# Retention and two MLPs on one core: tiles of their own for one half-depth product, GpSimd's sums in another order

## The chip, the core and the metric

The kernel runs on one core of a Trainium2 chip. Its engines work side by side, each through its own queue in order: TensorE (PE in the profile) multiplies, VectorE (DVE), ScalarE (ACT) and GpSimd (POOL) do the elementwise work, SyncE (SP) issues the transfers. Semaphores order work between engines. The metric is the device time of one execution in microseconds; lower is better.

## The reference

Per head a state decays and takes in one token; the result, of 1536 tokens by 512, goes through two MLPs with a hidden width of 2048. All is float32.

```
state = gamma * state + k_t v_t^T ;  y_t = q_t state / sqrt(64)     # 2 x 8 heads, 768 tokens, 64 wide
h = x @ w_in ;  g = max(h, 0) + log1p(exp(-|h|)) ;  x = g @ w_out    # layer 0 (softplus)
h = x @ w_in2 ; g = s * max(h, 0)^2 + b ;           y = g @ w_out2   # layer 1
```

## The kernel before

**Products in three parts.** TensorE multiplies a short format, so every operand is split in a high part (ScalarE copies it, rounding) and a low part (GpSimd or VectorE subtracts the high part): wh and wl of the weights, gh and gl of the hidden values, xh and xl of the inputs. A product is high x high, high x low and low x high. Tokens lie in three tiles of 512 (j = 0, 1, 2); the hidden width in 16 blocks of 128. The first product of a block (12 matmuls of 128x512) makes h; the curve makes g; the second product (`acc_mm`, `acc_2`, 12 matmuls into four accumulator banks) adds to the output, and VectorE reads the banks out into xa (`take_2`, L591). The first group's readout is ScalarE's (`take_out`, L412).

**The weights.** `split_w` makes one half of a block's weights from raw words: four VectorE operations in two pairs (L287 and L291, then L296 and L302), a square on ScalarE (L294), and at the next slot wh on ScalarE and wl on GpSimd (L112, L115). An ordered list (`halves`, made by `pair`) says which half comes next; each slot of the program (`part`) takes one from it, up to a limit, and `go(work, 2)` issues it in two pieces.

**Layer 0** runs in this order: twelve steps (blocks 0 to 3 for each j; the last four, 8 to 11, after retention is over), a plain part (`plain`, blocks 4 and 5, six slots k = 0 to 5), three pairs of blocks by `second` (pairs 3, 4, 5), and twelve steps more (36 to 47). Layer 1 is a plain part and seven pairs.

**A pair** (`second`) saves products: with j = 0 and 1 and the two halves of depth it needs seven half-depth products (`six`, 6 matmuls) instead of eight. For these it needs sums of x (x1 to x4, made once by `sum_x0`, split by `parts_x`) and four sums of weights (`sums_w`, ws, on GpSimd; `split_sums` makes sh and sl). Its six slots are, with TensorE's work: (2) two products for c11, second product; (3) two products with sums of weights, second product; (4) two products for c12 and c22, second product; (5) one for c21, second product; (6) 12 matmuls for ha (j = 2), second product; (7) 12 for hb, second product. The second products in (2) to (5) belong to the pair before.

**The curve** of layer 0 in a pair: r = max(h, 0) on ScalarE (`begin`, L534); u = h - 2r = -|h| on VectorE (`middle`, L546); softplus of u on ScalarE (L547); c = r + u on GpSimd (`finish`, L555). The split into gh and gl is issued a slot later (`end_part`). In the plain part and the steps the curve is three operations: VectorE, ScalarE, VectorE (L536, L539, L559 and L360, L366, L370). c and u come from a ring of four tiles (`next_t`: t1 and t2, two each).

Of the kernel before, what the change touches and what calls it, by code (L numbers as in the profile page):

```python
# [7 lines left out]
F32 = mybir.dt.float32  # L8
# [40 lines left out]
def tile_retention_mlps(ctx: ExitStack, tc: tile.TileContext, qk, kv, w1, w2, sb, consts, out):  # L49
# [401 lines left out]
    def sum_x0(k):  # L451

        def of(j, half):
            return [t[j][:, 2 * half : 2 * half + 2].bitcast(F32) for t in (xh, xl)]

        def put(op, to, x, y):
            nc.vector.tensor_tensor(out=to, in0=x, in1=y, op=op)

        add, less = ALU.add, ALU.subtract
        (h11, l11), (h12, l12), (h21, l21), (h22, l22) = of(0, 0), of(1, 0), of(0, 1), of(1, 1)  # L460
        if k > 2:
            h, l = (h22, l22) if k == 3 else (h21, l21)
            for c, tag in enumerate(("p5", "u2")):
                t = x3[c] = late.tile([P, TT], F32, tag=tag, name=tag)
                put(less, t, h[:, c], (h12 if k == 3 else x_t[2])[:, c])
            yield
            for c in range(2):
                put(add, x3[c], x3[c], l[:, c])
                if k == 3:
                    put(less, x3[c], x3[c], l12[:, c])  # L470
            yield
            return
        t = x_t[k] = xa[2][:, 2 * k - 2 : 2 * k]
        put(less, t, h12 if k == 1 else h22, h11 if k == 1 else x_t[1])
        yield
        put(add, t, t, l12 if k == 1 else l22)
        yield
        if k == 1:
            put(less, t, t, l11)
            yield  # L480

    def parts_x(k, la=1):
# [40 lines left out]
        nc.vector.tensor_tensor(out=c, in0=ps, in1=t, op=ALU.add)  # L523
        return c

    def begin(la, src, own=False, by_pool=True):

        if la:
            c = src if own else next_t()
            nc.scalar.activation(c, src, AF.Relu)  # L530
            return src, c, None
        r = next_t()
        if by_pool:
            nc.scalar.activation(r, src, AF.Relu)  # L534
            return src, r, src if own else next_t()
# [76 lines left out]
    def pair(la, p):  # L612
        w = la * NF + 2 * p
        at[la, p] = len(halves)
        if p != (0 if la else P0):
            return [(w, 0), (w + 1, 0), (w, 2), (w, 1), (w, 3), (w + 1, 1)]
        return [(w, 0), (w + 1, 0), (w, 1), (w + 1, 1)]

    for p in range(P0, P1):
# [12 lines left out]
    def load_next():  # L632
        x = next(loads, None)
        if x:
            load_w(*x)

    def split_next(to):
# [5 lines left out]
        if x[1] == 2:  # L643
            return sums_w(x[0])
        if x[1] == 3:
            return split_sums(x[0])
# [62 lines left out]
    with tc.manual_schedule():  # L709
# [146 lines left out]
        def plain(la, p, left, sums, parts):  # L856

            w = la * NF + 2 * p
            base = at[la, p + 1]
            accs = left + [lambda: whole(*of_pair(la, p, 0, 0)), lambda: whole(*of_pair(la, p, 0, 1)), lambda: None]  # L860
            banks = [(ps_h, "h"), (ps_y, "y"), None, (ps_h, "h"), None, (ps_y, "y")]
            for k, (j, half) in enumerate((j, half) for j in range(NTILE) for half in range(2)):
                part(base + k + 2)
                to = bank(*banks[k]) if banks[k] else bank_2[1]
                all_of(to, w_t[w + half, 0], j)
                if la and k == 2:
                    end_part()
                    accs[k]()
                of = begin(la, to, by_pool=False)
                if not la:  # L870
                    end_part()
                    go(work, 2)
                finish(la, p, half, j, of)
                if la:
                    end_part()
                if not la or k != 2:
                    accs[k]()
                go(work, 4 if la else 2)
                for x in sums[k]:
                    next(x, None)  # L880
                for x in parts[k]:
                    parts_x(x, la)

        def second(la, p):
# [16 lines left out]
            six(third, a12, b21, True)  # L901
            c11 = begin(la, joined(third, p1), own=True)
            end_part()
            go(work, 2)
            middle(c11)
            whole(*of_pair(la, p - 1, 1, 0))
            finish(la, p, 0, 0, c11)
            go(work, 2)

            part(base + 3)  # L910
            six(other, s1, t1, True)
# [1 line left out]
            six(one, s2, t2, False)  # L913
            u2 = kept(one, "u2")
            end_part()
            go(work, 2)
            whole(*of_pair(la, p - 1, 1, 1))
            go(work, 2)

            part(base + 4)  # L920
            six(other, s4, b22, False)
# [4 lines left out]
            go(work, 2)  # L926
# [32 lines left out]
            go(work, 2)  # L959
# [17 lines left out]
        sums_0 = all_x0()  # L977
        for s in range(SB, GS):
            accs = [of_step(s - LAG)]
            step(s, accs, at[0, P0 + 1] * (s < SB + 2), [sums_0] * max(1, s - SB), nc.gpsimd)  # L980
        s = GS - 1
        act_3(s)
        act_hi(s)
        act_lo(s, nc.gpsimd)
        parts_x(1, 0)
        left = [lambda s=s: whole(*of_step(s)) for s in range(GS - LAG, GS)]
        plain(0, P0, left, [[], [], [sums_0], [sums_0], [], []], [(2,), (4,), (), (), (3,), ()])
        for p in range(P0 + 1, P1):
            second(0, p)
        end_part()  # L990
# [103 lines left out]
```

## Time and profile before

| | |
|---|---|
| median of 3 runs | 594.05 us (591.74 to 594.84) |
| the profiled execution | 594.36 us, its span 592.3 us |
| TensorE, VectorE, ScalarE, GpSimd busy | 570.2, 418.7, 337.1, 329.4 us |
| TensorE's granted clock, mean | 0.986 of full speed |

TensorE is the engine that sets the time. A timeline row gives the start, how long the instruction (or a run of like ones, with its count) took, and in brackets the idle time before it with the instruction that ended it. Matmul records overlap: each shows 0.39 us and starts 0.23 after the one before it.

### The profile page before, as it was taken

The page shows a single profiled execution, that of the slowest core. Times are in us where ns is not written, and L with a number is a line of the kernel's source. Part 1 is how long each engine was busy: PE and PEld are TensorE (multiplying, and loading weights), DVE is VectorE, ACT ScalarE, POOL GpSimd, SP SyncE. Part 2 cuts the span into 40 slices and gives each one's busy share as a digit, 9 for nine tenths or more (in the row PEclk, how much of TensorE's full clock was granted, in tenths as well). Part 3 has the DMA queues.
Part 4 walks back from the last instruction along what each step waited for, and adds up shares of the span by engine and source line. Part 5 has one row for each costly group of instructions (what it writes and reads, how often), then busy time and mean ns, then how long its engine had stood idle before and what let it go on. Part 6 is the DMA issues. An engine that isn't in the chain of part 4 may idle for free.

```text
span 592.3 us, 8095 instructions
## 1 busy us (share of the span) xinstructions
PE 570.2 (96%) x2968; PEld 466.6 (79%) x2968; DVE 418.7 (71%) x628; ACT 337.1 (57%) x606; POOL 329.4 (56%) x266
## 2 busy tenths in 40 slices
PE   8889999999969979899999999999999999999997
PEld 7767878877858858688888887888888888888886
DVE  4898768889956749988786778657667575765324
ACT  4655563454544454643253788777666666767470
POOL 3447632767875686761043759846465555647130
PEclk9999999998989989899999999999999999999999
DMA  8986122121212212232121213131212212100005
GB/s 335 413 308 197 48 72 71 37 71 37 71 36 71 71 37 71 82 101 68 35 72 35 72 35 107 36 108 35 89 53 72 72 58 85 37 0 1 0 1 213
DMA packets 14870, 50.58 MB, mean 85 GB/s; under 512 B 1776, under 2 KB 1776, under 8 KB 14832
## 3 DMA queue, kind: packets, MB, share of 16 engines
q1 hardware_dynamic: 14832, 50.08, 24.6%
q8 instruction: 23, 0.38, 0.3%
q14 instruction: 15, 0.12, 0.1%
HBM read 46.93 MB, written 3.15 MB: 85 GB/s over the span
## 4 chain that ended last, share of the span: by engine, by line
PE 56%; POOL 4%; ACT 2%; DVE 2%; issue 1%; DVEq 0%; POOLq 0%; ACTq 0%
PE acc L581 25%; PE h L498 6%; PE acc L404 5%; PE y L506 5%; PE third L506 4%; PE y L498 3%; PE h L353 3%; PE y L353 3%; PE third L498 2%; POOL gl L115 1%; DVE xa L591 1%; POOL c L555 1%; POOL wl L115 1%; PE h L506 0%; ACT c L553 0%
## 5 line engine op out<-in xcount | busy, mean ns | idle before, releaser
L115 POOL TENSOR_TENSOR wl<-wm,wh 128x512 fp32r<-128x512 f32 x64 | 86.4, 1350 | 119.9 <-ACT wh L112 119.9
L115 POOL TENSOR_TENSOR gl<-c,gh 128x512 fp32r<-128x512 f32 x72 | 94.4, 1314 | 101.2 <-ACT gh L112 87.5
L591 DVE TENSOR_TENSOR xa<-acc,xa 128x512 f32<-128x512 f32 x132 | 82.4, 684 | 84.0 <-PE acc L581 83.9
L581 PE MATMUL acc<-wh,gh 128*128 128x512 f32 x192 | 74.9, 390 | 0.0
L581 PE MATMUL acc<-wh,gl 128*128 128x512 f32 x192 | 74.7, 389 | 0.0
L112 ACT ACTIVATE gh<-c 128x512 fp32r<-128x512 f32 x72 | 45.5, 632 | 12.7 <-POOL c L555 8.6
L581 PE MATMUL acc<-wl,gh 128*128 128x512 f32 x192 | 52.5, 389 | 0.0
L581 PE MATMUL acc<-gh,wh 128*128 128x512 f32 x96 | 39.9, 416 | 12.0 <-DVE xa L591 10.2
L112 ACT ACTIVATE wh<-wm 128x512 fp32r<-128x512 f32 x64 | 39.8, 622 | 18.0 <-DVE wm L302 18.0
L294 ACT ACTIVATE wm<-raw 128x512 f32<-128x512 f32 x64 | 42.1, 658 | 2.6 <-POOL ws L321 1.7
L581 PEld LDWEIGHTS acc<-wh,gh 128*128 128x128 f32 x192 | 36.0, 188 | 8.2 <-DVE xa L591 0.4
L302 DVE SCALAR_TENSOR_TENSOR wm<-wm,word 128x512 f32<-128x512 f32 x54 | 37.2, 688 | 7.3 <-ACT wm L294 1.5
L291 DVE SCALAR_TENSOR_TENSOR word<-raw,cu,word 128x512 uint32<-128x512 uint32 x54 | 40.8, 756 | 1.9
L581 PEld LDWEIGHTS acc<-wl,gh 128*128 128x128 f32 x192 | 36.1, 188 | 7.5
L581 PEld LDWEIGHTS acc<-wh,gl 128*128 128x128 f32 x192 | 36.0, 188 | 7.4
L296 DVE SCALAR_TENSOR_TENSOR word<-raw,cu,word 128x512 uint32<-128x512 uint32 x54 | 40.5, 751 | 0.8
L553 ACT ACTIVATE c<-c,sbt 128x512 f32<-128x512 f32 x48 | 39.2, 818 | 1.6
L581 PE MATMUL acc<-gl,wh 128*128 128x512 f32 x96 | 39.9, 416 | 0.0
L404 PE MATMUL acc<-gh,wh 128*128 128x512 f32 x96 | 38.3, 399 | 0.0
L404 PE MATMUL acc<-gl,wh 128*128 128x512 f32 x96 | 37.5, 390 | 0.0
L287 DVE TENSOR_SCALAR word<-raw 128x512 uint32<-128x512 uint32 x54 | 37.1, 687 | 0.4
L530 ACT ACTIVATE c<-c 128x512 f32<-128x512 f32 x21 | 13.3, 633 | 42.0 <-DVE c L523 41.4
(213 smaller groups left out, 1405.0 us busy)
## 6 DMA issues: line engine op xcount, KB each, us to landing
raw<-w SPq DMA_DIRECT2D x64, 512.0 KB, 3.7
qk<-qk SPq DMA_DIRECT2D x12, 512.0 KB, 7.8
kv<-kv SPq DMA_DIRECT2D x12, 512.0 KB, 7.9
out<-xa SPq DMA_DIRECT2D x12, 256.0 KB, 2.1
cst<-consts SPq DMA_DIRECT2D x1, 518.0 KB, 4.2
cst<-consts SPq DMA_DIRECT2D x1, 256.0 KB, 5.4
sbt<-sb SPq DMA_DIRECT2D x1, 1.0 KB, 10.6
```

Source lines behind the costliest of these rows:

```text
L112: nc.scalar.activation(hi, src, AF.Copy)
L115: lo_eng.tensor_tensor(out=lo, in0=src, in1=hi.bitcast(F32), op=ALU.subtract)
L291: nc.vector.scalar_tensor_tensor(out=x, in0=hw, scalar=cu[:, 0:1], in1=x, op0=ALU.bitwise_and, op1=ALU.bitwise_or)
L294: nc.scalar.activation(m, hw.bitcast(F32), AF.Square)
L296: nc.vector.scalar_tensor_tensor(out=x, in0=lw, scalar=cu[:, 1:2], in1=x, op0=ALU.logical_shift_right, op1=ALU.bitwise_or)
L302: nc.vector.scalar_tensor_tensor(out=m, in0=m, scalar=TINY_SQ, in1=x.bitcast(F32), op0=ALU.is_ge, op1=ALU.mult)
L404: nc.tensor.matmul(acc_t[la, g, j][cc], *ops[i], start=f4 == 0 and i == 0, stop=ends(s) and i == 2)
L498: nc.tensor.matmul(ps, w[a][:, k * P : (k + 1) * P], x[b][:, k], start=start and i == 0, stop=i == len(ops) - 1, skip_group_check=True,)
L506: nc.tensor.matmul(ps, w[a][:, k * P : (k + 1) * P], (xh, xl)[b][j][:, k], start=i == 0, stop=i == len(ops) - 1)
L553: nc.scalar.activation(c, c, AF.Identity, scale=sbt[:, 0:1], bias=sbt[:, 1:2])
L581: nc.tensor.matmul(acc_t[la, p, "pair", j][cc], *ops[i], start=half == 0 and i == 0, stop=half == 1 and i == 2)
L591: nc.vector.tensor_tensor(out=dst, in0=ps, in1=dst, op=ALU.add)
```

## The change

c21's two curve tiles no longer come from the ring of four: they lie in the places of u2 and p1, two tiles of the pair that hold copied-out products. GpSimd's sums of weights (`sums_w`, `split_sums`) are issued at the end of a slot, behind the curve's sums, and in layer 0's list the second sum step stands ahead of the second half of a block's weights. The plain part's blocks 0 and 1 take no weights, so all later halves of layer 0 come two slots later; steps 36 to 39 take one in every slot. x's first sum goes from VectorE (three operations of 128x1024) to GpSimd (six of 128x512); x3 is made from x2; x4 and x3 are summed behind blocks 0 and 1. The gl of steps 36 to 39 goes to GpSimd.

```diff
         if k > 2:
-            h, l = (h22, l22) if k == 3 else (h21, l21)
...
+            t, t2 = x3, x_t[2]
+            todo = ((t2, h11, less), (None, l11, less)) if k == 3 else ((h21, t2, less), (None, l21, add))
+            for x, y, op in todo:
+                for c in range(2):
+                    nc.vector.tensor_tensor(out=t[c], in0=t[c] if x is None else x[:, c], in1=y[:, c], op=op)
             return
         t = x_t[k] = xa[2][:, 2 * k - 2 : 2 * k]
         if k == 1:
-            put(less, t, t, l11)
+            for x, y, op in ((h12, h11, less), (t, l12, add), (t, l11, less)):
+                for c in range(2):
+                    nc.gpsimd.tensor_tensor(out=t[:, c], in0=x[:, c], in1=y[:, c], op=op)
+                yield
...
-    def begin(la, src, own=False, by_pool=True):
+    def begin(la, src, own=False, by_pool=True, tags=None):
...
+        if tags:
+            r, u = (late.tile([P, TT], F32, tag=tag, name=tag) for tag in tags)
...
-            return [(w, 0), (w + 1, 0), (w, 2), (w, 1), (w, 3), (w + 1, 1)]
+            return [(w, 0), (w + 1, 0), (w, 2)] + [(w, 1), (w, 3)][:: 1 if la else -1] + [(w + 1, 1)]
...
+        def go_first():
+            if work not in sums_of_w:
+                go(work, 2)
+
+        def go_last():
+            go(work, 4 if work in sums_of_w else 2)
...
-                part(base + k + 2)
+                part(base + k + 2 if la or k > 1 else 0)
...
-            c21 = begin(la, one)
+            c21 = begin(la, one, tags=("u2", "p1"))
             end_part()
-            go(work, 2)
+            go_first()
...
-            step(s, accs, at[0, P0 + 1] * (s < SB + 2), [sums_0] * max(1, s - SB), nc.gpsimd)
+            step(s, accs, at[0, P0 + 1] * (s < SB + 2), [sums_0], nc.gpsimd)
...
-        plain(0, P0, left, [[], [], [sums_0], [sums_0], [], []], [(2,), (4,), (), (), (3,), ()])
+        plain(0, P0, left, [[sums_0], [sums_0], [], [], [], []], [(4,), (2,), (), (3,), (), ()])
...
-            step(s, accs, 0 if k < 4 and k % 2 or k > 4 and ends(s - LAG) else lim)
+            step(s, accs, 0 if k > 4 and ends(s - LAG) else lim, lo=nc.gpsimd if k < 5 else None)
```

Three places show the order of the instructions. ScalarE in pair 4, slots 4 and 5 before (c_2026 and c_2036 are the curves of c12 and c22, c_2074 is c21's tile, h_1918 its product, gh_2077 c12's high part; the brackets name the engines it waits for):

```order
L112 ACTIVATE wh0_1994<-wm_1996 128x512
L547 ACTIVATE c_2026<-c_2026 128x512 [waits DVE_49]
L547 ACTIVATE c_2036<-c_2036 128x512 [waits DVE_49]
L534 ACTIVATE c_2074<-h_1918 128x512 [waits PE_49,Pool_49]
L112 ACTIVATE gh_2077<-c_2028 128x512
```

and now (u2_2056 is c21's tile, h_1897 its product):

```order
L294 ACTIVATE wm_2021<-raw_1759 128x512 [waits DMAHW7_49,Pool_49]
L546 ACTIVATE c_2003<-c_2003 128x512 [waits DVE_49]
L546 ACTIVATE c_2013<-c_2013 128x512 [waits DVE_49]
L533 ACTIVATE u2_2056<-h_1897 128x512 [waits PE_49]
L112 ACTIVATE gh_2059<-c_2005 128x512 [waits Pool_49]
```

c21's first curve instruction no longer waits for GpSimd; c12's high part, behind it, now does.

GpSimd in pair 4 before, from slot 3's weights to the sums' low part (c x2 are c12 and c22, the next c is c21):

```order
L115 TENSOR_TENSOR wl_1945<-wm,wh_1944 128x512
L115 TENSOR_TENSOR wl_1995<-wm,wh_1994 128x512
L321 TENSOR_TENSOR ws<-wm 128x256
L321 TENSOR_TENSOR ws<-ws,wm 128x256
L321 TENSOR_TENSOR ws<-wm 128x256
L321 TENSOR_TENSOR ws<-wm,ws 128x256
L555 TENSOR_TENSOR c<-c 128x512 x2
L115 TENSOR_TENSOR gl<-c,gh 128x512 x2
L555 TENSOR_TENSOR c<-c 128x512
L115 TENSOR_TENSOR gl<-c,gh 128x512
L115 TENSOR_TENSOR wl_2086<-wm,wh_2085 128x512
L115 TENSOR_TENSOR sl<-ws,sh 128x1024
```

and now, from c21's sum (u_2056) to the sums' low part (the c's are ha and hb):

```order
L554 TENSOR_TENSOR u_2056<-u_2056,p_2057 128x512
L115 TENSOR_TENSOR gl<-u_2056,gh 128x512
L115 TENSOR_TENSOR wl_2070<-wm,wh_2069 128x512
L554 TENSOR_TENSOR c<-c 128x512
L321 TENSOR_TENSOR ws<-wm 128x256
L321 TENSOR_TENSOR ws<-ws,wm 128x256
L321 TENSOR_TENSOR ws<-wm 128x256
L321 TENSOR_TENSOR ws<-wm,ws 128x256
L115 TENSOR_TENSOR gl<-c,gh 128x512
L554 TENSOR_TENSOR c<-c 128x512
L115 TENSOR_TENSOR sl<-ws,sh 128x1024
```

The sums of weights moved from ahead of c12 and c22 to behind ha, two slots later.

VectorE from x2's last sum to the plain part's block 1, before (p and u are x4's tiles; the word and wm rows are weights):

```order
L457 TENSOR_TENSOR xa_111<-xa_111,xl_107 128x1024
L457 TENSOR_TENSOR p_1344<-xh_103,xa_111 128x512
L457 TENSOR_TENSOR u_1346<-xh_103,xa_111 128x512
L457 TENSOR_TENSOR p_1344<-p_1344,xl_106 128x512
L457 TENSOR_TENSOR u_1346<-u_1346,xl_106 128x512
L536 TENSOR_SCALAR c<-h 128x512
L287 TENSOR_SCALAR word<-raw 128x512
L291 SCALAR_TENSOR_TENSOR word<-raw,cu,word 128x512
L559 SCALAR_TENSOR_TENSOR c<-h,c 128x512
L296 SCALAR_TENSOR_TENSOR word<-raw,cu,word 128x512
L302 SCALAR_TENSOR_TENSOR wm<-wm,word 128x512
L536 TENSOR_SCALAR c<-y 128x512
```

and now (p_1389, u_1390 are x4's tiles, p_1434, u_1435 x3's):

```order
L474 TENSOR_TENSOR xa_111<-xh_104,xa_111 128x1024
L475 TENSOR_TENSOR xa_111<-xa_111,xl_107 128x1024
L535 TENSOR_SCALAR c<-h 128x512
L558 SCALAR_TENSOR_TENSOR c<-h,c 128x512
L465 TENSOR_TENSOR p_1389<-xh_103,xa_111 128x512
L465 TENSOR_TENSOR u_1390<-xh_103,xa_111 128x512
L465 TENSOR_TENSOR p_1389<-p_1389,xl_106 128x512
L465 TENSOR_TENSOR u_1390<-u_1390,xl_106 128x512
L535 TENSOR_SCALAR c<-y 128x512
L558 SCALAR_TENSOR_TENSOR c<-y,c 128x512
L465 TENSOR_TENSOR p_1434<-xa_111,xh_103 128x512
L465 TENSOR_TENSOR u_1435<-xa_111,xh_103 128x512
```

x4's sums moved behind block 0's curve, and x3's follow block 1's where weights stood.

## Rows read from the trace of the kernel before

**Rows 1.** The page: engines' shares. Then TensorE's waits: us in total, times, longest us.
```profile
PE 570.2 (96%) x2968; PEld 466.6 (79%) x2968; DVE 418.7 (71%) x628; ACT 337.1 (57%) x606; POOL 329.4 (56%) x266
...
PE acc L581 <- DVE xa L591: 10.2, 3, 4.2
```

**Rows 2.** TensorE's timeline: start us, us, instruction, count, idle before and its releaser.
```profile
134.36 0.50 PE L581 MATMUL acc<-gh,wh 128*128 128x512 f32 x1 [1.79 <-ACT xa L412]
...
141.59 0.39 PE L581 MATMUL acc<-gh,wh 128*128 128x512 f32 x1
...
175.27 0.77 PE L581 MATMUL acc<-gh,wh 128*128 128x512 f32 x1 [4.25 <-DVE xa L591]
...
180.40 0.40 PE L506 MATMUL y<-xh,wh 128*128 128x512 f32 x1
...
213.05 0.47 PE L581 MATMUL acc<-gh,wh 128*128 128x512 f32 x1 [3.91 <-DVE xa L591]
...
220.21 0.39 PE L581 MATMUL acc<-gh,wh 128*128 128x512 f32 x1
...
248.21 0.51 PE L581 MATMUL acc<-gh,wh 128*128 128x512 f32 x1 [2.00 <-DVE xa L591]
...
252.62 0.39 PE L506 MATMUL y<-xh,wh 128*128 128x512 f32 x1
...
255.34 0.39 PE L581 MATMUL acc<-gh,wh 128*128 128x512 f32 x1
...
369.04 0.50 PE L498 MATMUL y<-xh,sh 128*128 128x512 f32 x1 [1.26 <-ACT p L512]
```

**Rows 3.** Two stretches: us, each engine's busy us, granted clock, DMA share, GB/s.
```profile
245.00:253.00 8.00, 6.00 (x20) 4.50 (x19) 7.04 (x12) 4.64 (x9) 7.26 (x6) 0.79 0.32 104
367.00:373.00 6.00, 4.74 (x21) 3.62 (x20) 4.27 (x8) 3.75 (x7) 5.92 (x7) 1.00 0.25 87
```

**Rows 4.** Waits between 100 and 262 us: us in total, times, longest us.
```profile
DVE c L546 <- POOL gl L115: 13.8, 3, 6.5
...
ACT c L534 <- POOL c L555: 13.0, 4, 4.5
```

**Rows 5.** GpSimd's timeline in layer 0's pairs 4 and 5.
```profile
204.24 0.74 POOL L321 TENSOR_TENSOR ws<-wm 128x256 f32<-128x256 f32 x1
...
207.15 2.52 POOL L555 TENSOR_TENSOR c<-c 128x512 f32<-128x512 f32 x2
...
217.55 2.38 POOL L115 TENSOR_TENSOR sl<-ws,sh 128x1024 fp32r<-128x1024 f32 x1
...
240.05 1.82 POOL L115 TENSOR_TENSOR wl<-wm,wh 128x512 fp32r<-128x512 f32 x1 [4.01 <-ACT wh L112]
```

**Rows 6.** VectorE's timeline in layer 0's pair 5.
```profile
233.55 2.48 DVE L591 TENSOR_TENSOR xa<-acc,xa 128x512 f32<-128x512 f32 x4 [0.25 <-PE acc L581]
...
237.44 0.68 DVE L523 TENSOR_TENSOR c<-y,u 128x512 f32<-128x512 f32 x1
...
240.02 2.39 DVE L546 SCALAR_TENSOR_TENSOR c<-c 128x512 f32<-128x512 f32 x2
...
246.18 0.69 DVE L546 SCALAR_TENSOR_TENSOR c<-c,h 128x512 f32<-128x512 f32 x1 [0.79 <-POOL gl L115]
```

**Rows 7.** GpSimd's and VectorE's timelines beside each other, in steps 10 and 11.
```profile
109.49 1.96 POOL L115 TENSOR_TENSOR wl<-wm,wh 128x512 fp32r<-128x512 f32 x1 [3.52 <-ACT wh L112]
...
117.95 3.44 POOL L492 TENSOR_TENSOR x1l<-xa,x1h 128x512 fp32r<-128x512 f32 x2
...
118.46 1.77 DVE L457 TENSOR_TENSOR u<-xh,xa 128x512 f32<-128x512 f32 x1
...
121.85 0.68 DVE L457 TENSOR_TENSOR u<-u,xl 128x512 f32<-128x512 f32 x1
```

**Rows 8.** VectorE's and ScalarE's timelines in the plain part's block 2.
```profile
130.54 0.68 DVE L536 TENSOR_SCALAR c<-third 128x512 uint32<-128x512 uint32 x1
...
133.24 2.04 ACT L412 ACTIVATE xa<-acc 128x512 f32<-128x512 f32 x4
```

More of the change, by code (lines that the diff above doesn't have):

```diff
@@ L454, in of @@
             return [t[j][:, 2 * half : 2 * half + 2].bitcast(F32) for t in (xh, xl)]
-        def put(op, to, x, y):
-            nc.vector.tensor_tensor(out=to, in0=x, in1=y, op=op)
         add, less = ALU.add, ALU.subtract
@@ L461, in sum_x0 @@
         if k > 2:
-            h, l = (h22, l22) if k == 3 else (h21, l21)
             for c, tag in enumerate(("p5", "u2")):
[L464 to L471, printed above, removed]
+                x3[c] = late.tile([P, TT], F32, tag=tag, name=tag)
+            t, t2 = x3, x_t[2]
[3 more added lines that the diff above has]
+                    nc.vector.tensor_tensor(out=t[c], in0=t[c] if x is None else x[:, c], in1=y[:, c], op=op)
             return
         t = x_t[k] = xa[2][:, 2 * k - 2 : 2 * k]
[L474 to L477, printed above, removed]
         if k == 1:
-            put(less, t, t, l11)
+            for x, y, op in ((h12, h11, less), (t, l12, add), (t, l11, less)):
+                for c in range(2):
+                    nc.gpsimd.tensor_tensor(out=t[:, c], in0=x[:, c], in1=y[:, c], op=op)
+                yield
+        else:
+            nc.vector.tensor_tensor(out=t, in0=h22, in1=x_t[1], op=less)
+            nc.vector.tensor_tensor(out=t, in0=t, in1=l22, op=add)
             yield
@@ L531, in begin @@
             return src, c, None
-        r = next_t()
+        if tags:
+            r, u = (late.tile([P, TT], F32, tag=tag, name=tag) for tag in tags)
+        else:
+            r, u = next_t(), None
         if by_pool:
             nc.scalar.activation(r, src, AF.Relu)
-            return src, r, src if own else next_t()
+            return src, r, u if tags else src if own else next_t()
         nc.vector.tensor_scalar(
@@ L635, in load_next @@
             load_w(*x)
+    sums_of_w = []
     def split_next(to):
@@ L642, in split_next @@
         nxt[0] = next(splits, None)
[L643 to L646, printed above, removed]
+        if x[1] > 1:
+            sums_of_w.append((sums_w, split_sums)[x[1] - 2](x[0]))
+            return sums_of_w[-1]
         return split_w(*x, pause=True)
@@ L907, in second @@
             finish(la, p, 0, 0, c11)
-            go(work, 2)
+            go_last()
             part(base + 3)
@@ L915, in second @@
             end_part()
-            go(work, 2)
+            go_first()
             whole(*of_pair(la, p - 1, 1, 1))
-            go(work, 2)
+            go_last()
             part(base + 4)
@@ L925, in second @@
             end_part()
-            go(work, 2)
+            go_first()
             middle(c12)
@@ L931, in second @@
             finish(la, p, 1, 1, c22)
-            go(work, 2)
+            go_last()
             part(base + 5)
             six(one, a22, n4, False)
-            c21 = begin(la, one)
+            c21 = begin(la, one, tags=("u2", "p1"))
             end_part()
-            go(work, 2)
+            go_first()
             middle(c21)
@@ L941, in second @@
             finish(la, p, 1, 0, c21)
-            go(work, 2)
+            go_last()
             part(base + 6)
@@ L947, in second @@
             end_part()
-            go(work, 2)
+            go_first()
             middle(ha)
@@ L951, in second @@
             finish(la, p, 0, 2, ha)
-            go(work, 2)
+            go_last()
             part(base + 7)
@@ L958, in second @@
             end_part()
-            go(work, 2)
+            go_first()
             middle(hb)
@@ L964, in second @@
             finish(la, p, 1, 2, hb)
-            go(work, 2)
+            go_last()
         def all_x0():
-            for k in (1, 2, 4):
+            for k in (1, 2, 4, 3):
                 yield from sum_x0(k)
-            yield from sum_x0(3)
+                if k > 2:
+                    yield
         def all_x():
```

## The prediction, made before the changed kernel was run

> **What bounds the kernel now.** I read the engines' shares first, then what TensorE waits for, then its timeline at each of those waits. TensorE is busy for 570.2 of 592.3 us, so the change can only pay where TensorE stands still or runs slowly. Three of its waits, 10.2 us together, are for VectorE's readout of the accumulators (L591) [rows 1]. They are the 4.25, 3.91 and 2.00 us in layer 0's pairs 3, 4 and 5, each ahead of the second layer's first product of that pair; a fourth of 1.79 us, for ScalarE's readout (L412), stands in the plain part [rows 2].
>
> Each of the four costs more than its idle time. Twelve matmuls take 2.72 us (252.62 to 255.34). After the 4.25 us the next twelve take 5.13 (175.27 to 180.40), 2.41 too many; after the 3.91 the next 24 take 7.16 instead of 5.44 (1.72 more); after the 2.00 twelve take 4.41 (1.69 more); after the 1.79, 24 take 7.23 (1.79 more) [rows 2]. The granted clock tells why: 0.79 on the mean of 245 to 253 us, so part of it at 1.2 of 2.4 GHz, against 1.00 in 367 to 373, where TensorE had been idle for only 1.26 [rows 2, 3]. In sum the three pairs lose 10.16 + 5.82 = 15.98 us and the plain part 3.58: 19.6 us is what there is to gain.
>
> Now who holds VectorE up: its wait in the curve of c21 for GpSimd's gl, 13.8 us in three times, and ahead of it ScalarE's wait for GpSimd's c, 13.0 us in four [rows 4]. c21 takes its two tiles from a ring of four whose next entries still belong to c12; GpSimd reaches c12 only behind the weights' four sums (204.24 to 207.15, 2.91 us) [rows 5]. The readout of the accumulators is queued behind c21 on VectorE, and TensorE's next product behind that readout.
>
> **Own tiles for c21.** In the changed order c21's first ScalarE instruction waits for TensorE alone. The two tiles are free by then: p1 was read by c11's sum, u2 by c12's sum just ahead. So the wait goes, and VectorE's own queue is next. The two-slot shift gives all three pairs the VectorE order that only pair 5 had, with a weight part in each of the first four slots, so pair 5 prices them. It began at 248.21 - 2.00 - 23.12 (102 matmuls at 2.72 for twelve) = 223.09. VectorE reads out at 233.55, forms c12 and c22 from 237.44, holds the two curve steps at 240.02 for 2.39 us (a GpSimd weight part runs from 240.05 to 241.87 beside them) and could start c21's at 246.18 - 0.79 = 245.39 [rows 5, 6]. TensorE then starts at 248.21 - 0.79 = 247.42, where it was ready at 246.21: 1.21 us of idle stay, from backlog on VectorE alone. Bounds: 0 if the two curve steps do not meet a weight part (some 1.2 us less), 2.0 as pair 5 shows. I take 1.21 in each pair, being the row with one wait taken out, and no loss of clock, since 1.26 of idle had none [rows 2, 3]; 1.7 each if it has.
>
> **Weights' sums behind the curves' sums, weights later.** GpSimd's c12 and c22 come free 2.91 us sooner, which helps nobody once c21 has tiles of its own. The price is at the other end: the sums' low parts (sl) of the next pair are now made ahead of its fifth matmul on them by little. From 240.05 in pair 5's count (16.96 after the pair's start): the weight part 1.82, eleven operations of 128x512 at 1.26 (207.15: 2.52 for two), the sums 2.91, sl 2.38, and 0.74 waiting for gh plus about 0.3 of sharing (estimates from the same stretch) give 39.0 [rows 5]. TensorE wants sl at 31.28 (138 matmuls) + 1.21 + 5.44 + 0.91 = 38.8. I take 0.3 us for each of pairs 4 and 5; 0 to 2 are its bounds, one GpSimd operation more or less. c11's sum also waits now for gl of the last curve, about 0.3 us, which VectorE's wait of 0.25 and the rest of its slack before the readout hide [rows 6]; without that cover 0.3 more. Pairs after: 3 x 1.21 + 2 x 0.3 = 4.2 us, a gain of 11.8.
>
> **x's first sum on GpSimd, x's other sums, no weights in blocks 0 and 1.** Six operations of 128x512 at 1.26 go to GpSimd, which waits for 3.52 us there [rows 5, 7]; VectorE loses three of 128x1024, two of the last six sums, and two weight parts of four operations. But x2 needs the last of them. GpSimd: 109.49 + 1.26 (weight part) + 1.26 (gl) + 2.52 = 114.5. From there VectorE's sums, all from SBUF to SBUF, run beside a busy GpSimd, and rows 7 show how: the 128x512 sum at 118.46 takes 1.77 and ends 0.56 after GpSimd's first operation of the pair at 117.95 (1.72 each); with GpSimd idle at 121.85 it takes 0.68. They alternate, 1.7 us a turn. So: x2, two of 128x1024, 2 x 2.24 (twice 0.54, plus 1.16; an estimate from these rows) to 119.0; block 0's three curve steps 2.0, to 121.0; x4's four, half of them held, 3.8, to 124.8; block 1's curve 1.9, to 126.7; x3's four, all held, since they wait for x4l (same tiles) and x2l follows on GpSimd, 6.3, to 133.0. There block 2's curve begins, which began at 130.54 before [rows 8]. Behind it: 0.6, two weight operations 1.4, 0.6, gh 0.6, and two readouts of 0.51 (133.24: 2.04 for four) with 0.1: TensorE starts at 137.3 [rows 8]. It is ready at 134.36 - 1.79 = 132.57 [rows 2]: 4.7 us of idle, and 2.0 for the clock (between 1.72 and 2.41): 6.7 where 3.58 were, a loss of 3.1. Bounds: all of x4 and x3 free (0.6 each) brings TensorE's start to 132, no idle at all; all held, 7.6 and 2.4.
>
> The Trainium skill (GPSIMD Engine Reference, 3.1 Elementwise) says that a two-input sum takes about twice as long on GpSimd as on VectorE and that such work belongs on VectorE. The ratio is that of 1.26 to 0.62 [rows 5, 6]. By that rule alone the six moved operations would cost 3.8 us and the sum would be 589.5; by the trace GpSimd is idle there, and it is x2's start that counts.
>
> **Layer 0's last four steps and layer 1.** Two weight parts and the turn of gl to GpSimd in steps 36 to 39: VectorE has about 4 x 2.8 (weight parts) + 8 x 0.62 (readouts) + 8 x 0.62 (curves) = 21.1 us of work in TensorE's 21.8. TensorE needs each readout a step later, 2 us after it ends; I cost it at nothing, at most 2. In layer 1 sl moves behind one gl, 1.26 us, with its matmuls a whole pair away: nothing. The loads follow their weight parts and keep their lead of four.
>
> **Sum.** The execution took 594.36 us (span 592.3), 0.3 over the median. 594.36 - 11.8 + 3.1 = **585.7 us**.
>
> **Rivals.**
> (A) The plain part gets no worse. For it: the alternation needs GpSimd busy at every turn. Cost there 0 to 3.6 instead of 6.7: 579.0 to 582.6; with the pairs' backlog gone too, 574.8.
> (B) The shorter stalls still drop the clock, 1.69 to 1.79 being the price even after 1.79 of idle: 585.7 + 3 x 1.7 = 590.8, and 593.2 if the pairs keep 2.0 us each. Against it: 1.26 of idle at 1.00 [rows 2, 3].
> (C) The GpSimd time itself lands on the path: 589.5. It is the Trainium skill's rule above. Against it: 3.52 of idle [rows 7].
> (D) Slower: sl becomes the bound in pairs 4 and 5. If VectorE's sums hold each of the twelve operations ahead of sl by 0.54, sl is 6.5 late, with 1.7 for the clock, twice: 602. It decides from 8.7 / 2 = 4.4 us a pair, clock included. Against it: VectorE's work in that stretch reads mostly PSUM.
> (E) c21 stays blocked by some other tile, so that nothing is gained: 594.4.
>
> **Chances.** The forecast 0.47, with its own range 583 to 589; A 0.21, B 0.18, C 0.05, D 0.06, E 0.03. A range of 579 to 592 leaves out D, E, a third of B and A's lowest end (0.05), about 0.2. Half a per cent of 594.05, 3.0 us, is what a measurement here can tell from no change: under 591.1 lie the forecast, A, C and half of B (0.82); within it the rest of B and E (0.12); above it D (0.06).
>
> **What would show it.** VectorE's curve step of c21 without a wait for GpSimd, and TensorE's waits for L591 at about 1.2 us, with granted clock 1.00 behind them, prove the first step; idle of 2 us or more there, or a clock under 1.00, prove B. The wait for L412 in the plain part at 4 to 5 us, with VectorE's x3 sums at 1.7 us each, proves the third; a wait under 1.8 proves A. TensorE waiting for sl by more than 1 us in pairs 4 and 5 would make D, and the forecast too low.

## The result and the profile after

The changed kernel takes 586.22 us (median of 4 runs, 585.01 to 586.59), the kernel before 594.38 beside it: a ratio of 0.9872, interval 0.9843 to 0.9901. The forecast was 585.7. The profiled execution took 586.1 us with a span of 584.0, 8.3 less than the 592.3 of before. One execution of a later kernel, tiles_defer, ran at a granted clock of 0.558 throughout and took 941.03 us; it stands in no median here, and its trace is not read.

First the page, its line of engines (busy us, share, instructions), then TensorE's waits (us in total, times, longest):

```profile
PE 565.4 (97%) x2968; PEld 462.7 (79%) x2968; DVE 411.0 (70%) x619; ACT 337.5 (58%) x606; POOL 340.8 (58%) x276
...
PE acc L580 <- ACT xa L412: 5.1, 1, 5.1
PE acc L580 <- DVE xa L590: 3.3, 3, 1.1
```

Against [rows 1] the wait for VectorE's readout (L591 there, L590 here) fell from 10.2 to 3.3 us, and the wait for ScalarE's readout in the plain part is now the longest. TensorE's timeline (start, us, instruction, idle before it and its releaser), the rows that answer to [rows 2]:

```profile
137.90 0.80 PE L580 MATMUL acc<-gh,wh 128*128 128x512 f32 x1 [5.05 <-ACT xa L412]
...
142.80 0.39 PE L502 MATMUL third<-xh,wh 128*128 128x512 f32 x1
...
175.36 0.47 PE L580 MATMUL acc<-gh,wh 128*128 128x512 f32 x1 [1.11 <-DVE xa L590]
...
189.74 0.39 PE L494 MATMUL y<-x1l,sh 128*128 128x512 f32 x1
190.23 0.73 PE L494 MATMUL y<-x1h,sl 128*128 128x512 f32 x2
190.81 0.39 PE L494 MATMUL h<-x2h,sh 128*128 128x512 f32 x1
...
208.38 0.47 PE L580 MATMUL acc<-gh,wh 128*128 128x512 f32 x1 [1.09 <-DVE xa L590]
...
241.47 0.47 PE L580 MATMUL acc<-gh,wh 128*128 128x512 f32 x1 [1.09 <-DVE xa L590]
...
244.31 0.39 PE L502 MATMUL y<-xh,wh 128*128 128x512 f32 x1
```

The windows (start and end, us, each engine's busy us, granted clock, DMA share, GB/s) give the clock of the plain part and behind each pair's stall:

```profile
128.00:145.00 17.00, 11.95 (x44) 9.42 (x43) 13.37 (x16) 7.83 (x14) 11.28 (x8) 0.80 0.19 63
173.00:181.00 8.00, 6.88 (x31) 5.41 (x30) 5.36 (x9) 4.28 (x8) 7.26 (x6) 1.00 0.34 110
206.00:214.00 8.00, 6.91 (x31) 5.41 (x30) 5.38 (x9) 4.32 (x8) 7.26 (x6) 1.00 0.36 112
239.00:247.00 8.00, 6.91 (x31) 5.41 (x30) 7.66 (x13) 5.07 (x9) 7.26 (x6) 1.00 0.35 113
```

Now the account closes. Idle is counted as the profile shows it, from the end of the last matmul's record. Pairs: 1.11 + 1.09 + 1.09 = 3.29 us of idle at full clock, plus sl in pairs 4 and 5. There the starts 189.74, 190.23, 190.81 are 0.49 and 0.58 apart where 0.23 and 0.45 would do without a wait, so 0.39 in pair 4; in pair 5, 33 us later, the gaps are 0.48 and 0.58. Together 4.1 where 15.98 were, a gain of 11.9. Plain part: 5.05 of idle, and twelve matmuls in 4.90 us (137.90 to 142.80) instead of 2.72, so 7.2 where 3.58 were, a loss of 3.65. The balance, 8.3, is the difference of the spans. From pair 5's second product on nothing moved: 584.0 - 244.31 = 339.7 us to the end, 592.3 - 252.62 = 339.7 before.

### The profile page after: what moved, and what is told of

Same layout as the page of the kernel before. It is cut to its first block, busy times and chain, and to the rows that moved or that the text cites. A ratio compares the mean times of both kernels' runs of the same rounds, so it can differ in the third digit from the quotient of the medians.

```text
span 584.0 us, 8106 instructions
## 1 busy us (share of the span) xinstructions
PE 565.4 (97%) x2968; PEld 462.7 (79%) x2968; DVE 411.0 (70%) x619; ACT 337.5 (58%) x606; POOL 340.8 (58%) x276
## 4 chain that ended last, share of the span: by engine, by line
PE 76%; DVE 12%; POOL 3%; ACT 3%; DMA 3%; issue 2%; DVEq 0%; SPq 0%; ACTq 0%
PE acc L580 28%; PE acc L404 10%; PE h L494 7%; PE h L353 6%; PE y L502 6%; PE third L502 4%; PE y L353 4%; PE y L494 4%; PE y L190 2%; PE third L494 2%; DMA qk<-qk 2%; DVE xa L590 2%; POOL sl L115 1%; DVE c L545 1%; PE s L174 1%
## 5 line engine op out<-in xcount | busy, mean ns | idle before, releaser
L115 POOL TENSOR_TENSOR wl<-wm,wh 128x512 fp32r<-128x512 f32 x64 | 84.8, 1325 | 109.8 <-ACT wh L112 109.8
L115 POOL TENSOR_TENSOR gl<-c,gh 128x512 fp32r<-128x512 f32 x69 | 91.2, 1323 | 87.1 <-ACT gh L112 69.1
L590 DVE TENSOR_TENSOR xa<-acc,xa 128x512 f32<-128x512 f32 x132 | 82.4, 684 | 84.2 <-PE acc L580 84.2
L112 ACT ACTIVATE gh<-c 128x512 fp32r<-128x512 f32 x69 | 43.6, 632 | 11.0 <-POOL c L554 6.7
L580 PE MATMUL acc<-gl,wh 128*128 128x512 f32 x96 | 38.4, 400 | 0.0
L404 PE MATMUL acc<-gl,wh 128*128 128x512 f32 x96 | 37.5, 390 | 0.0
```

The lines of the kernel that those rows point to most:

```text
L112: nc.scalar.activation(hi, src, AF.Copy)
L115: lo_eng.tensor_tensor(out=lo, in0=src, in1=hi.bitcast(F32), op=ALU.subtract)
L404: nc.tensor.matmul(acc_t[la, g, j][cc], *ops[i], start=f4 == 0 and i == 0, stop=ends(s) and i == 2)
L580: nc.tensor.matmul(acc_t[la, p, "pair", j][cc], *ops[i], start=half == 0 and i == 0, stop=half == 1 and i == 2)
L590: nc.vector.tensor_tensor(out=dst, in0=ps, in1=dst, op=ALU.add)
```

## Experiments

All are compared with the kernel before, which took 594.38 us beside the changed kernel and 593.60 to 594.09 beside the others; the medians stand beside the longest idle times of TensorE (us, from each kernel's own trace; a blank means none). In the last column the waits are for VectorE's readout, but for gl in pairs 3 and 4 of b_tiles, a_early and tiles_order.

| kernel | median | ratio, interval | plain part | pair 3, sl | pairs 3, 4, 5 |
|---|---|---|---|---|---|
| before | 594.38 | | 1.79 | | 4.25, 3.91, 2.00 |
| changed | 586.22 | 0.9872, 0.9843 to 0.9901 | 5.05 | | 1.11, 1.09, 1.09 |
| b_tiles | 582.93 | 0.9818, 0.9788 to 0.9848 | 1.78 | | 0.86, 0.85, 1.41 |
| a_ring | 589.62 | 0.9932, 0.9909 to 0.9955 | 5.05 | | 2.01, 1.97, 1.97 |
| a_sums_first | 585.24 | 0.9857, 0.9828 to 0.9886 | 5.05 | | 1.11, 1.19, 1.21 |
| a_early | 590.92 | 0.9959, 0.9942 to 0.9976 | 7.06 | | 2.41, 2.25, 1.12 |
| a_x_before | 586.31 | 0.9871, 0.9841 to 0.9901 | | 3.74 | 1.11, 1.09, 1.08 |
| a_x3_late | 584.44 | 0.9839, 0.981 to 0.9869 | | 3.45 | 1.11, 1.08, 1.09 |
| tiles_order | 588.43 | 0.9911, 0.9877 to 0.9945 | 1.79 | | 2.40, 2.27, 1.11 |
| a_x3_later | 580.46 | 0.9787, 0.9764 to 0.9809 | | 1.00 | 1.45, 1.18, 1.25 |

### The tiles alone, and everything but the tiles

b_tiles is the kernel before with this edit:

```diff
-            c21 = begin(la, one)
+            c21 = begin(la, one, tags=("u2", "p1"))
```

> The kernel before with one edit: c21 gets tiles of its own (u2 and p1). Order of weights, of GpSimd's sums and of x's sums stays that of before.
> Theory (the two ring tiles alone make the pairs' stalls): in pairs 3 and 4 VectorE waited 6.5 us for gl against TensorE's 4.25 and 3.91 of idle, so both idle times go to 0; in pair 5 1.21 us stay (2.00 less the wait of 0.79); the clock stays 1.00 behind them; the plain part stays at 1.79 + 1.79. 594.4 - 16.0 + 1.2 = 579.6 us, less than the changed kernel's 586.2.
> Rival (GpSimd's weight sums ahead of its curve sums hold the path as well): 1 to 2.9 us of idle stay in pairs 3 and 4, with or without the lower clock: 582 to 589.
> Rival (VectorE's backlog is what counts, and with early weights it is another one): about 1.2 us in each of the three, 583.

582.93 us, so the tiles alone give 11.2 us, more than the whole change gives; the runs (582.84 to 584.07) lie wholly under the changed kernel's (585.01 to 586.59). The long stalls for the readout are gone in pairs 3 and 4, and something new stands a product later. TensorE's timeline there:

```profile
179.08 0.50 PE L584 MATMUL acc<-gl,wh 128*128 128x512 f32 x1 [0.86 <-POOL gl L115]
...
211.93 0.50 PE L584 MATMUL acc<-gl,wh 128*128 128x512 f32 x1 [0.85 <-POOL gl L115]
...
239.52 0.47 PE L584 MATMUL acc<-gh,wh 128*128 128x512 f32 x1 [1.41 <-DVE xa L594]
```

By starts of matmuls, which lie closer than the ends of their records, these three cost 1.12, 1.13 and 1.58 us, where the expectation had 0, 0 and 1.2; another 1.4 us of the profiled run lies in its first 25 us, in waits for the loads of the inputs. The gl waited for is that of c21 itself, which GpSimd makes last (177.75 us). The tiles freed VectorE, and then c21's own chain on GpSimd was next. The time is that of the third expectation, 583, but in pairs 3 and 4 the wait is GpSimd's, as the second had it.

a_ring is the changed kernel with the same edit taken back.

> The changed kernel with one edit undone: c21 takes its two tiles from the ring of four again; GpSimd's sums behind the curves' sums, weights later and x's sums stay as changed.
> Theory (every pair now has the order that pair 5 had before, and the tiles are what remained): VectorE waits some 0.8 us for gl ahead of c21's curve step in pairs 3, 4 and 5, TensorE is idle 2.0 us in each, and the clock falls behind it, 1.7 us each: 586.2 + 3 x 2.5 = 593.7.
> Rival (moving GpSimd's sums was enough, the tiles are idle): no wait for gl, 1.1 us in each pair: 586.2.
> Rival (the clock does not fall at 2.0 us of idle): 588.8.

589.62 us (588.52 to 591.89). VectorE waits 0.79 us for gl in each of the three pairs, and TensorE stands 2.01, 1.97 and 1.97 us, where the theory had some 0.8 and 2.0. Its price for the clock was too high. Windows of this kernel behind the three stalls:

```profile
174.00:182.00 8.00, 5.99 (x27) 4.64 (x26) 5.03 (x8) 3.75 (x7) 7.25 (x7) 1.00 0.24 79
208.00:216.00 8.00, 6.05 (x20) 4.83 (x21) 4.94 (x8) 3.27 (x6) 7.26 (x6) 0.79 0.21 72
243.00:251.00 8.00, 6.03 (x27) 4.96 (x27) 7.65 (x12) 4.14 (x8) 6.86 (x7) 1.00 0.23 74
```

In this execution only one of three equal stalls was followed by the lower clock. The mean granted clock of the seven runs, 0.988 to 0.994, suggests that the number differs from run to run.

### GpSimd's order and the weights' slots

a_sums_first takes GpSimd's order within a slot back in the changed kernel, in all six slots of a pair (the order of the list stays as changed, and no run here takes that back alone):

```diff
-            go_first()
+            go(work, 2)
...
-            go_last()
+            go(work, 2)
```

> The changed kernel with one edit undone: GpSimd's weight sums stand ahead of its curve sums again, in the slots as they come; tiles, late weights and x's sums stay as changed.
> Theory (with c21's own tiles nothing on the path waits for the curve sums as long as VectorE's backlog of 1.1 us is there): pairs 3 to 5 unchanged or up to 1.1 us longer in pairs 3 and 4 for gl, sl 0.39 sooner in pairs 4 and 5: 585.4 to 587.6.
> Rival (the order of the sums was needed): 3 us and more a pair: 592 or more.

585.24 us, 1.0 less than the changed kernel by the medians (the intervals overlap, so the difference is not shown). TensorE's readout waits are 1.11, 1.19 and 1.21, and the 0.39 us for sl in pairs 4 and 5 are gone from its timeline. With c21's own tiles the new order of GpSimd gains TensorE 0.2 us of readout waits in this kernel and costs it 0.8 us for sl.

a_early gives blocks 0 and 1 their weight parts back:

```diff
-                part(base + k + 2 if la or k > 1 else 0)
+                part(base + k + 2)
```

tiles_order does that and puts x's sums back as well (`sum_x0`, `all_x0` and the lists of before), so that the tiles, GpSimd's order and the edits to steps 36 to 39 are what is left of the change.

> The changed kernel with one edit undone: blocks 0 and 1 of the plain part take a weight part each again (weights not later); tiles, GpSimd's order and x's sums stay as changed.
> Theory: in the pairs the two slots give back VectorE's backlog in pairs 3 and 4 and sl's lateness (1.27 + 1.24 + 2 x 0.39 = 3.3 us less); in the plain part eight weight operations of 0.7 us more stand on VectorE ahead of block 2's curve, so the wait of 5.05 grows, by up to 5.6: 586.2 - 3.3 + 5.6 = 588.5, at least 583 if the plain part stays as it is.
> Rival (the weights' place is indifferent to the pairs): 586 to 592.

> The changed kernel with two edits undone, x's sums and the weights a slot later: c21's own tiles and GpSimd's weight sums behind its curve sums stay.
> With the tiles alone (582.9) TensorE lost 1.12 us in pair 3 and 1.13 in pair 4 waiting for gl, which GpSimd makes behind the weights' four sums (2.9 us).
> Theory (the order of GpSimd's sums is worth those 2.25 us, and with the weights in the early slots sl still comes in time): 580.7.
> Rival (the sums moved back make sl late, as in the changed kernel): 581.5 with 0.4 in each pair, up to 586 with 3.5 and the lower clock.
> Rival (the 1.1 us are VectorE's or the readouts' and stay): 582.9.

590.92 and 588.43 us, both above what the theories gave. GpSimd's timeline in pair 3 of tiles_order:

```profile
172.21 0.75 POOL L321 TENSOR_TENSOR ws<-wm 128x256 f32<-128x256 f32 x1
...
175.14 2.55 POOL L115 TENSOR_TENSOR gl<-c,gh 128x512 fp32r<-128x512 f32 x2
177.64 1.30 POOL L558 TENSOR_TENSOR u<-u,p 128x512 f32<-128x512 f32 x1
178.90 2.38 POOL L115 TENSOR_TENSOR sl<-ws,sh 128x1024 fp32r<-128x1024 f32 x1
181.23 1.27 POOL L115 TENSOR_TENSOR gl<-u,gh 128x512 fp32r<-128x512 f32 x1
```

and TensorE's:

```profile
182.56 0.50 PE L584 MATMUL acc<-gl,wh 128*128 128x512 f32 x1 [2.40 <-POOL gl L115]
```

With the weights in the early slots the new order puts sl (2.38 us) ahead of c21's gl, and TensorE stands 2.40 us for it; a_early shows 2.41 at the same place. So the order needs the late slots. tiles_order also waits 1.07 and 2.05 us at pair 3's start for the curves of the plain part's last blocks; there sl, moved ahead in the list, meets x3's sums (last section). In a_early the plain part's wait grew from 5.05 to 7.06, as forecast in kind: the late slots are also what kept the plain part from worse.

### The plain part

a_x_before puts x's sums back where they stood before. a_x3_late leaves x1 on GpSimd and moves x3's sums, by the formula of before, behind blocks 2 and 3 (and its parts x3h and x3l behind block 4):

```diff
-        plain(0, P0, left, [[sums_0], [sums_0], [], [], [], []], [(4,), (2,), (), (3,), (), ()])
+        plain(0, P0, left, [[sums_0], [], [sums_0], [sums_0], [], []], [(4,), (2,), (), (), (3,), ()])
```

> The changed kernel with one edit undone: x's four sums stand on VectorE and in the steps and blocks where they stood before (x's first sum on VectorE, x2 and x4 in the steps, x3 in halves behind blocks 2 and 3); tiles, GpSimd's order and later weights stay as changed.
> Theory (x's sums in the new places are what delays block 2's curve): TensorE's wait for ScalarE's readout in the plain part, 5.05 us and 2.18 us of clock behind it now, goes to 0 (VectorE has two weight parts less than before, where 1.79 were left) and the pairs stay: 579.0; if the 1.79 and its clock stay, 582.6.
> Rival (the late weights or the taken tiles delay the plain part, not the sums): 584 to 587.

> The changed kernel with x3's sums (four operations, now six, from x's parts alone) moved from behind block 1 to behind blocks 2 and 3, as halves; x's first sum stays on GpSimd, x2 and x4 stay where the change put them.
> Theory (four x3 sums at 1.7 us each, ahead of block 2's curve on VectorE, make the wait of 5.05 us): block 2's curve begins at about 127 instead of 133.5 and the wait goes to 0 to 1.8 us; 586.2 - 7.2 = 579.0, or 582.6 with 1.8 and the lower clock.
> Rival (GpSimd's x1 sums, for which x2 waits, start the delay, and it lasts): 3 us or more of idle stay: 584 to 586.

In both the wait of 5.05 us is gone, wholly, so x's sums did make it, and by a_x3_late it was x3's place. But the times are 586.31 and 584.44, not 579. Both lie in the range of the rival, whose reason is wrong all the same: no idle is left in the plain part. TensorE's and GpSimd's timelines of a_x3_late show where the gain went:

```profile
153.62 0.72 PE L498 MATMUL y<-x1h,sl 128*128 128x512 f32 x2 [3.45 <-POOL sl L115]
```

```profile
143.34 1.30 POOL L115 TENSOR_TENSOR wl<-wm,wh 128x512 fp32r<-128x512 f32 x1 [4.47 <-ACT wh L112]
...
148.75 1.29 POOL L492 TENSOR_TENSOR x3l<-p,x3h 128x512 fp32r<-128x512 f32 x1
150.00 1.27 POOL L492 TENSOR_TENSOR x3l<-u,x3h 128x512 fp32r<-128x512 f32 x1
151.23 2.34 POOL L115 TENSOR_TENSOR sl<-ws,sh 128x1024 fp32r<-128x1024 f32 x1
```

Pair 3's sl is late. Two slots without weights made it so: tiles_order, which is a_x_before with weights in blocks 0 and 1 again, starts this sl at 142.57 us and TensorE does not wait for it; a_x_before starts it at 152.72, and TensorE waits 3.74 us. In the changed kernel the plain part's own stall had hidden that. GpSimd's and TensorE's timelines there:

```profile
153.62 2.41 POOL L115 TENSOR_TENSOR sl<-ws,sh 128x1024 fp32r<-128x1024 f32 x1 [0.49 <-ACT sh L112]
```

```profile
157.31 0.62 PE L494 MATMUL y<-x1h,sl 128*128 128x512 f32 x2
```

sl is done at 156.03, 1.28 us before TensorE takes it up, and TensorE had lost 7.2 us in the plain part.

a_x3_later follows from it: x3's parts go behind block 5, so that both x3l leave GpSimd's queue ahead of sl, and GpSimd's sums stand in their slots again.

```diff
-        plain(0, P0, left, [[sums_0], [], [sums_0], [sums_0], [], []], [(4,), (2,), (), (), (3,), ()])
+        plain(0, P0, left, [[sums_0], [], [sums_0], [sums_0], [], []], [(4,), (2,), (), (), (), (3,)])
```

> The changed kernel with x3's sums behind blocks 2 and 3 (as in the run before that had them there), and two more edits: x3's parts stand behind block 5 instead of behind block 4, so that pair 3's sl goes ahead of both x3l on GpSimd; and GpSimd's weight sums stand in their slots again, not behind the curves' sums (worth 0.8 us when undone alone).
> Theory (once the plain part no longer waits, GpSimd's queue up to pair 3's sl is next: two operations of 1.28 ahead of it made 2.5 of the 3.6 us, and the lower clock behind 3.45 us of idle 1.9 more): a wait of 1.0 us for sl in pair 3 at full clock, the pairs' 1.2 us each stay, no wait for sl in pairs 4 and 5: 584.4 - 2.5 - 1.9 - 0.8 = 579.2, less than with the tiles alone (582.9).
> Rival (x3's tiles are p5 and u2, and pair 3's own p5 and u2 now wait for x3l): the gain comes back there, 582 to 584.
> Rival (sl is not held by x3l but by sh on ScalarE, whose end is the later one): 583 to 584.

580.46 us (580.30 to 581.25), the fastest kernel here. TensorE's timeline:

```profile
150.77 0.73 PE L498 MATMUL y<-x1h,sl 128*128 128x512 f32 x2 [1.00 <-POOL sl L115]
...
170.46 0.47 PE L584 MATMUL acc<-gh,wh 128*128 128x512 f32 x1 [1.45 <-DVE xa L594]
```

The wait for sl is the 1.00 us of the expectation, at full clock. The 1.3 us it missed by are in pair 3: 1.45 of idle instead of 1.11, and 0.84 ahead of c21's product (161.91 us), where a_x3_late had no wait. Which of the two edits that a_x3_late does not have makes them is not shown.

### Three that did not pay

tiles_order_out adds one edit to tiles_order:

> The same kernel with one more edit: in the plain part's block 2 ScalarE reads out the accumulators of step 11 ahead of that block's curve and parts, not behind them.
> Theory (TensorE's wait in the plain part is for four readouts that stand behind block 2's curve on ScalarE, and for nothing else): the 1.95 us and the 1.8 of lower clock behind them go: 580.7 - 3.7 = 577.0.
> Rival (the readouts still end late, since TensorE's own products ahead of them end only then, 2.0 us of readout stay): 579 to 581.
> Rival (ScalarE's delay of block 2's curve by some 4 us comes out later, in block 3 or pair 3): 581 to 585.

```diff
-                if la and k == 2:
-                    end_part()
+                if k == 2:
+                    if la:
+                        end_part()
                     accs[k]()
                 of = begin(la, to, by_pool=False)
...
-                if not la or k != 2:
+                if k != 2:
                     accs[k]()
```

587.90 us (ratio 0.991, 0.9881 to 0.9939) against 588.43, no difference that these runs show. TensorE's wait for ScalarE's readout is gone, and at pair 3's start it waits 3.22 us for block 4's curve, which reads the "third" bank, and 0.49 for block 5's, where 1.07 and 2.05 stood:

```profile
148.20 0.50 PE L498 MATMUL third<-xh,wh 128*128 128x512 f32 x1 [3.22 <-DVE c L562]
```

The wait came back where the second rival had it, but not for its reason. VectorE ends block 4's curve at 148.1 us, and at 148.5 without this edit: nothing was delayed, TensorE only came to it sooner. VectorE's queue ahead of that curve, with x3's sums beside sl (last section), sets the time there.

The next two, tiles_defer and tiles_defer_skip:

> The kernel before with own tiles for c21, and with one more edit: GpSimd's four weight sums stand a part later, behind c12's and c22's sums and both their low parts gl, and ahead of c21's sum. The weights keep their slots, x's sums their places.
> In the kernel with the tiles alone (582.9) the weights' sums stood ahead of c12's sum (170.67 us) and TensorE waited 1.12 us in pair 3 and 1.13 in pair 4 for gl; with the sums between the curve sums and gl those waits were 2.68 and 2.44.
> Theory (what counts is what stands ahead of gl on GpSimd): gl comes 2.9 us sooner and both waits go, c21's sum and sl keep their times: 582.9 - 2.25 = 580.7; VectorE's readout then is next, with 0 to 0.5 us a pair: 581.7 at most.
> Rival (VectorE's third weight step, which waited 2.19 us for gl in pair 3, sets the pace): nothing gained, 582.9.
> Rival (sh on ScalarE waits longer for the sums and sl is late): 583 to 586.

> The kernel with own tiles and the weights' sums a part later, and no weight part in the slot of c12 and c22 in pair 5 (all later weight parts one slot on; steps 36 and 38 take one each as the changed kernel's do).
> In pair 5 VectorE ran without a gap up to its readout, with two curve steps of 2.39 us beside GpSimd's weight part, and TensorE waited 1.41 us.
> Theory (the backlog of VectorE is that weight part of 2.8 us and the meeting): the wait goes, 580.7 - 1.6 = 579.1.
> Rival (the meeting only moves to the next weight part): 580.2 to 580.7.
> Rival (the weights a slot on are late in steps 36 to 39): above 581.

```diff
+        def go_now():
+            if work not in sums_of_w:
+                go(work, 2)
...
-            go(work, 2)
+            go_now()
...
-            go(late_work, 1)
+            go(late_work, 2)
...
-            part(base + 4)
+            part(0 if not la and p == P1 - 1 else base + 4)
```

The last of these edits, and one by which steps 36 and 38 take a weight part each, are tiles_defer_skip's alone. tiles_defer took 584.01 us (583.90 to 584.33; ratio 0.9842, 0.9801 to 0.9884), 1.1 more than the tiles alone. Its stalls are read from tiles_defer_skip, which has the same order in pairs 3 and 4 (583.21; 0.983, 0.9788 to 0.9873). ScalarE's and TensorE's timelines there:

```profile
173.82 0.66 ACT L294 ACTIVATE wm<-raw 128x512 f32<-128x512 f32 x1 [4.08 <-POOL ws L321]
174.39 0.62 ACT L550 ACTIVATE p<-p 128x512 f32<-128x512 f32 x1
...
176.41 0.63 ACT L112 ACTIVATE gh<-u 128x512 fp32r<-128x512 f32 x1 [0.92 <-POOL u L558]
```

```profile
177.10 0.50 PE L584 MATMUL acc<-gh,wh 128*128 128x512 f32 x1 [0.57 <-ACT gh L112]
...
178.45 0.50 PE L584 MATMUL acc<-gl,wh 128*128 128x512 f32 x1 [0.85 <-POOL gl L115]
```

I had named the wrong gl: the wait is for c21's (gl<-u), not c12's. The deferred sums still read two weights' wm, of which there are two buffers, so the next weight's square waits for them on ScalarE, and c21's curve waits behind it. The weight part left out of pair 5 did remove the stall of 1.58 us that b_tiles has there, and 0.63 came back at 291 us (0.47 of it a wait for VectorE's readout). tiles_defer_out adds the early readout to tiles_defer:

> The same kernel, and ScalarE's four readouts of step 11 in the plain part's block 2 ahead of that block's curve instead of behind it.
> Theory (the wait of 1.94 us and the 1.5 of lower clock behind it go, and what block 2's curve loses on ScalarE, up to 4 us, is caught up before its bank is wanted): 580.7 - 3.4 = 577.3.
> Rival (as with GpSimd's sums in the other order, where 3.4 us came back as a wait for block 2's bank): 579 to 581.
> Rival (it costs more than it saves): above 581.

584.18 us (0.9846, 0.9811 to 0.9882): again nothing, with 1.94 us of waiting for block 4's curve in the "third" bank, and 0.56 for block 5's, in place of the 1.78 for the readout. Block 4's curve ends at 146.7 us with the early readout and at 146.8 in tiles_defer_skip without it.

## Why the prediction was right

**Own tiles for c21: right.** VectorE's timeline in pair 3, where [rows 6] had pair 5 of before:

```profile
168.06 2.39 DVE L545 SCALAR_TENSOR_TENSOR c<-c 128x512 f32<-128x512 f32 x2
...
173.33 0.68 DVE L545 SCALAR_TENSOR_TENSOR p<-u,h 128x512 f32<-128x512 f32 x1
173.93 2.48 DVE L590 TENSOR_TENSOR xa<-acc,xa 128x512 f32<-128x512 f32 x4
```

No wait stands before c21's step, and the pair of curve steps costs the same 2.39 us as in pair 5 of before. The idle that stays is 1.1 us a pair (1.21 forecast), at clock 1.00. a_ring shows the cause: with ring tiles the 0.79 us of waiting and the 2.0 of idle are back in every pair. The reason why all pairs would look like pair 5, the two-slot shift, is right too, and b_tiles shows the other side of it, which the prediction did not draw out: without the shift pairs 3 and 4 have no such backlog (c12's and c22's curve steps take 1.35 us there, and 2.39 in pair 5).

**GpSimd's sums behind the curves: right for pairs 4 and 5, lucky for pair 3.** "Helps nobody once c21 has tiles of its own" is what a_sums_first shows, and sl was late by 0.39 us against 0.3. For pair 3's sl the prediction has no term, and gives no reason for that. It came to nothing because the plain part's stall of 7.2 us lay ahead of it; with that stall gone pair 3's sl cost 3.45 us of idle in a_x3_late, where both x3l stand ahead of it, and 1.00 in a_x3_later, where they stand behind it.

**Plain part: right in mechanism and nearly in size.** 7.2 us against 6.7, the difference being 5.05 against 4.7 of idle and 2.18 against 2.0 for the clock. VectorE's chain, with the forecast's times 119.0 (x2 done), 121.0, 124.8, 126.7 and 133.0 (block 2's curve begins):

```profile
114.84 2.29 DVE L474 TENSOR_TENSOR xa<-xh,xa 128x1024 f32<-128x1024 f32 x1 [1.50 <-POOL xa L471]
...
119.30 0.68 DVE L535 TENSOR_SCALAR c<-h 128x512 uint32<-128x512 uint32 x1
...
121.28 1.05 DVE L465 TENSOR_TENSOR p<-xh,xa 128x512 f32<-128x512 f32 x1
...
125.16 0.68 DVE L535 TENSOR_SCALAR c<-y 128x512 uint32<-128x512 uint32 x1
...
127.14 1.33 DVE L465 TENSOR_TENSOR p<-xa,xh 128x512 f32<-128x512 f32 x1
128.39 1.78 DVE L465 TENSOR_TENSOR u<-xa,xh 128x512 f32<-128x512 f32 x1
130.09 1.78 DVE L465 TENSOR_TENSOR p<-p,xl 128x512 f32<-128x512 f32 x1
131.79 1.77 DVE L465 TENSOR_TENSOR u<-u,xl 128x512 f32<-128x512 f32 x1
133.49 0.68 DVE L535 TENSOR_SCALAR c<-third 128x512 uint32<-128x512 uint32 x1
```

Beside x3's sums GpSimd forms x4l, a gl and x2l, and each engine slows the other; in a_x3_late the same two x2l take 2.56 us, and x3's last sums, with GpSimd idle, 0.69:

```profile
129.59 3.43 POOL L488 TENSOR_TENSOR x2l<-xa,x2h 128x512 fp32r<-128x512 f32 x2
```

```profile
140.06 0.69 DVE L466 TENSOR_TENSOR u<-u,xl 128x512 f32<-128x512 f32 x1
```

The Trainium skill (SBUF — State Buffer, Who interferes with whom) says that a VectorE operation with two inputs in SBUF contends with a GpSimd operation that reads SBUF, and that the ports they share are an exclusive lock. The trace agrees: 1.78 us for a sum of 0.69 is its own time and most of a GpSimd operation of 1.28.

**GpSimd's six operations (rival C): not what decided.** The Trainium skill (GPSIMD Engine Reference, 3.1 Elementwise) has a two-input sum at about twice VectorE's time on GpSimd. The trace agrees: 1.27 us (2.54 for two at 112.27) against 0.68. But the six cost VectorE only a wait of 1.50 us at 114.84; what reached TensorE came from x3's place, since a_x3_late keeps x1 on GpSimd and has no plain stall.

**Steps 36 to 39 and layer 1 at nothing: right in sum,** 339.7 us behind pair 5 in both kernels; no run takes these edits back one by one.

**Rivals.** A and E did not happen, nor C. B did not at 1.1 us. D, sl as the bound, was placed in pairs 4 and 5 only. Its place is pair 3, and it waits behind the plain part: it decides as soon as that stall is removed (3.45 and 3.74 us). The prediction's rival A, 579.0 to 582.6 with a plain part no worse, left that out: a_x_before has such a plain part and took 586.31.

## What to carry to other kernels

When a block waits for ring buffers that its neighbours still hold, give it tiles of its own first and measure that alone: here it was worth more than the same edit together with three rearrangements around it. A stall that an edit creates can cover another edit's lateness, so before counting on its removal, compute when the next operand arrives. Keep two-input sums in SBUF on VectorE away from a busy GpSimd when something urgent stands behind them in the queue.

## What the runs showed of the hardware

- Idle of 1.8 to 2.4 us on TensorE was followed by a lower clock sometimes, not always: 5 of the 16 such stalls in the traces here. 1.97 us was followed by a mean of 0.79 in one pair of a_ring, and 2.01 and 1.97 by 1.00 in the other two. 1.78 us in b_tiles was followed by 0.83 (132 to 142 us), the 1.79 at the same place of tiles_order by 1.00, and so were its 2.40 and 2.27. Idle of 1.0 to 1.45 us was followed by none in any trace here, 3.22 us and more by it each time.
- Two sums of 128x512 on VectorE took 4.59 us in tiles_order beside the end of a gl and sl on GpSimd; sl, one operation of 128x1024, itself took 2.85 instead of 2.38. The same two sums took 1.41 in tiles_defer_skip, with GpSimd idle. The rows of tiles_order:

```profile
141.38 4.59 DVE L457 TENSOR_TENSOR u<-u,xl 128x512 f32<-128x512 f32 x2
```

```profile
142.57 2.85 POOL L115 TENSOR_TENSOR sl<-ws,sh 128x1024 fp32r<-128x1024 f32 x1
```
